# Scores written to PSUM in the key order of V's rows, with the permutation taken out of the normalisation

## The chip, the cores and the metric

The kernel runs on one core of one Trainium2 chip. The metric is the device time of one execution in microseconds. Times quoted are medians of runs in the fast state; ratios are the mean time of one kernel's fast runs over the mean of the other's fast runs of the same rounds, so they are not quite the ratio of the medians that stand beside them. Runs of one execution (called "one look") have no interval.

Names used below: PE is TensorE, ACT is ScalarE, DVE is VectorE, POOL is GpSimd, SP issues the loads. PV is the product of the probabilities with V, QP the Q projection; an evacuation copies a result out of PSUM. `L436` is line 436 of the kernel. In the profiles, SPq or ACTq is an engine's sequencer, and "issue" is time in which an engine waited for nothing that the profile shows.

## The reference

Two independent attention blocks, A and B, whose outputs are put side by side:

```python
def ref(x, k_cache, v_cache, wq, wo):       # x (16, 64, 640), caches (16, 32, 512, 128)
    q = (x @ wq).reshape(B, Sq, 32, 128).transpose(0, 2, 1, 3)
    scores = jnp.einsum("bhqd,bhkd->bhqk", q, k_cache) * 128 ** -0.5
    p = softmax(scores, axis=-1)            # over 512 keys
    o = jnp.einsum("bhqk,bhkd->bhqd", p, v_cache)
    return o.transpose(0, 2, 1, 3).reshape(B, Sq, 32 * 128) @ wo
```

All arrays are bf16. K and V of both blocks make up 268 MB of the 292 MB read.

The scores of these inputs are tiny (standard deviation near 0.001, worked out from the input scales), so the softmax is nearly uniform, and the comparison with the reference does not notice keys in a wrong order.

## The kernel before

Each pack is four heads of two batch rows; 128 packs follow each other. The kernel gives each engine a list of instructions, set out by hand, which it goes through in that order. Four pieces matter.

```python
# Loads: a partition of K holds 16 consecutive keys, a partition of V holds 4 consecutive keys.
src = K[...].rearrange("h (p t) d -> (h p) (t d)", t=16)     # key = 16 * k + j
src = V[...].rearrange("g (p t) d -> p g t d", p=128)        # key = 4 * p + t

def em_KT(e, op):       # DVE: 32x32 block transposes of K, 1024 fp32 (pairs of bf16) per partition
    dst = kt_ring[:, n % NKT, b].rearrange("p t j k two -> p (t j k two)").bitcast(F32)
    ins = e.transpose(dst, kn_ring[:, n % NK, b, :].bitcast(F32))

def em_S(e, op):        # PE: scores, 32 matmuls in four waves (f) of eight array tiles (b, i)
    for f in range(4):
        for b in range(2):
            for i in range(4):
                last = e.matmul(ps[64 * b:64 * b + 64, i, :], qs_ring[rows, n % NQ, f, b, :],
                                kt_ring[rows, n % NKT, b, :, f // 2, :, f % 2],
                                start=(f == 0), stop=(f == 3), tile_position=(32 * i, 64 * b))

def em_NM(e, op):       # POOL: p / rowsum, and the keys into the order of V's rows
    src = p_ring[:, h % NP, :].rearrange("q (th tl k) -> q th tl k", th=4, tl=4)
    dst = pn_ring[:, h % NPN, :].rearrange("q (tl k th) -> q th tl k", tl=4, th=4)
    ins = e.tensor_scalar(dst, src, recip[...], 1.0, ALU.mult, ALU.mult)
# ... (exponential on ACT, reciprocal and most evacuations on DVE, transposes of p, PV and projection on PE)
```

With j = 4 th + tl, a key is 16 k + 4 th + tl. The scores leave PE in the order (th, tl, k). V's row 4 k + th of chunk tl needs the order (tl, k, th). The normalisation therefore reads one contiguous row of 512 bf16 and writes neighbours four elements (8 bytes) apart.

## Time and profile before

951 us (median 950.95 of 4 runs, 948.79 to 951.89).

| | before |
|---|---|
| profiled span | 946.3 us |
| busy: PE / DVE / ACT / POOL | 741.5 / 577.9 / 418.6 / 700.1 us |
| start of the first normalisation | 47.4 us |
| distance of packs in the steady part | 6.73 us |
| the eight packs at the switch from block A to B | 77.2 us together |
| normalisation, start to start in a pair | 1.25 us |

The distance of packs is the time from the first normalisation of one pack to that of the next, taken from the trace's start times. Share of busy time alone would point at PE (78%) as much as at POOL (74%). The chain that ended last decides. This is its summary by engine on the page of before:

```profile
POOL 72%; DVE 11%; PE 10%; SPq 4%; issue 2%; DMA 1%; ACT 0%; ACTq 0%
```

And this is that chain in order of time in the steady part of before (columns: start us, length us, what; one pack is the stretch from one four-fold normalisation to the next):

```profile
307.69 5.17 POOL pn_ring L436 x4
312.87 0.05 issue
312.92 0.63 PE ps L444 x8
313.55 0.02 issue
313.57 0.69 DVE pT_ring L449
314.26 0.08 DVE recip L429
314.35 0.08 issue
314.43 5.17 POOL pn_ring L436 x4
```

Four normalisations take 5.17 us. Then the probabilities of the last two heads are transposed on PE, copied by DVE, and only then does DVE come to the reciprocal of the next pack, since it is behind that copy in DVE's list. From one to the next it is 6.74 us. The groups of before that the change touches (line, engine, operation, shapes, count; busy us, mean ns; idle time before and its cause):

```profile
L436 POOL TENSOR_SCALAR pn_ring<-p_ring,recip 128x512 bf16<-128x512 bf16 x512 | 662.9, 1417 | 195.9 <-DVE recip L429 195.9
L403 PE MATMUL ps<-kt_ring,qs_ring 32*64 32x512 bf16 x4096 | 146.9, 398 | 1.9 <-DVE kt_ring L393 1.9
```

The mean of 1417 ns for a normalisation contains overlap with the next one; start to start it is 1.25 us.

### The profile page before, as it was taken

How to read it: one execution, taken by the hardware profiler on the slowest of the kernel's cores; microseconds unless marked ns; L12 is line 12 of the kernel's file. 1: busy time of each engine (PE TensorE's matmuls, PEld its weight loads, DVE VectorE, ACT ScalarE, POOL GpSimd, SP SyncE). 2: the span in 40 equal slices, each digit the busy share in tenths (PEclk: the TensorE clock that was granted, in tenths of full speed). 3: DMA queues.
4: the chain of work that ended last, by engine and by line, in shares of the span. 5: the costliest groups of instructions: out<-in, count | busy, mean ns of one | idle time of the engine just before them, and what ended most of it. 6: DMA issues, size and time to landing. Idle time of an engine off the chain costs nothing.

```text
span 946.3 us, 31604 instructions
## 1 busy us (share of the span) xinstructions
PE 741.5 (78%) x13905; PEld 524.2 (55%) x13905; DVE 577.9 (61%) x902; ACT 418.6 (44%) x1313; POOL 700.1 (74%) x550
## 2 busy tenths in 40 slices
PE   3077888888888888887677888888888888888884
PEld 2055556565656565655455565656565656555553
DVE  2056666666666666666445666666666666666663
ACT  1034545444544444444333454545454444454442
POOL 2099777777777778788777878787878777777774
PEclk9999999999999999999989999999999999999999
DMA  9999999989999998997579999999999999999820
GB/s 332 366 368 342 367 325 307 336 305 330 318 327 312 318 331 307 324 362 271 199 236 377 373 375 378 376 372 327 327 315 319 325 311 332 305 334 317 300 86 12
DMA packets 195729, 296.79 MB, mean 314 GB/s; under 512 B 9216, under 2 KB 162816, under 8 KB 195584
## 3 DMA queue, kind: packets, MB, share of 16 engines
q1 hardware_dynamic: 193280, 292.06, 89.4%
q10 hardware_dynamic: 2304, 2.62, 0.8%
q8 instruction: 112, 1.84, 0.8%
q14 instruction: 33, 0.27, 0.1%
HBM read 292.03 MB, written 2.62 MB: 311 GB/s over the span
## 4 chain that ended last, share of the span: by engine, by line
POOL 72%; DVE 11%; PE 10%; SPq 4%; issue 2%; DMA 1%; ACT 0%; ACTq 0%
POOL pn_ring L436 68%; DVE pT_ring L449 9%; PE ps L444 8%; POOL wqp_sb L357 2%; POOL wqp_sb L356 1%; SPq L349 1%; SPq L335 1%; DVE recip L429 1%; PE ps L380 1%; DMA ws_ring<-in_A_wq_dram 1%; SPq L342 1%; DVE kt_ring L393 1%; DVE qs_ring L386 0%; PE ps L403 0%; PE ps L460 0%
## 5 line engine op out<-in xcount | busy, mean ns | idle before, releaser
L436 POOL TENSOR_SCALAR pn_ring<-p_ring,recip 128x512 bf16<-128x512 bf16 x512 | 662.9, 1417 | 195.9 <-DVE recip L429 195.9
L416 ACT ACTIVATE p_ring<-ps 128x512 bf16<-128x512 f32 x512 | 304.0, 596 | 358.7 <-PE ps L403 358.7
L449 DVE COPY pT_ring<-ps 128x1024 bf16<-128x1024 bf16 x256 | 177.1, 692 | 294.7 <-PE ps L444 294.7
L393 DVE STREAM_TRANSPOSE kt_ring<-kn_ring 128x1024 f32<-128x1024 f32 x256 | 315.9, 1234 | 7.5 <-DMA kn_ring<-in_A_k_cache_dram 7.5
L444 PE MATMUL ps<-ident,pn_ring 128*128 128x128 bf16 x2048 | 159.9, 221 | 184.6 <-POOL pn_ring L436 184.6
L444 PEld LDWEIGHTS ps<-ident,pn_ring 128*128 128x128 bf16 x2048 | 116.0, 98 | 238.5 <-POOL pn_ring L436 238.1
L460 PEld LDWEIGHTS ps<-pT_ring,v_ring 128*128 128x128 bf16 x4096 | 141.2, 99 | 58.5 <-issue 57.5
L380 PE MATMUL ps<-xT_ring,wqp_sb 128*128 128x128 bf16 x2560 | 170.9, 224 | 2.1 <-POOL wqp_sb L357 1.3
L474 PE MATMUL ps<-wo_sb,oT_ring 128*128 128x512 bf16 x512 | 167.6, 385 | 0.0
L460 PE MATMUL ps<-pT_ring,v_ring 128*128 128x64 bf16 x4096 | 165.1, 194 | 2.7 <-DVE pT_ring L449 1.7
L466 ACT ACTIVATE oT_ring<-ps 128x256 bf16<-128x256 f32 x256 | 98.3, 384 | 143.4 <-PE ps L460 143.4
L380 PEld LDWEIGHTS ps<-xT_ring,wqp_sb 128*128 128x128 bf16 x2560 | 156.8, 115 | 3.3 <-ACT p_ring L416 1.7
L403 PE MATMUL ps<-kt_ring,qs_ring 32*64 32x512 bf16 x4096 | 146.9, 398 | 1.9 <-DVE kt_ring L393 1.9
L386 DVE TENSOR_SCALAR qs_ring<-ps 128x512 bf16<-128x512 f32 x128 | 88.5, 692 | 52.6 <-PE ps L380 52.6
L477 PE MATMUL ps<-wo_sb,oT_ring 128*128 128x128 bf16 x512 | 112.4, 220 | 0.0
L416 ACT ACTIVATION_READ_ACCUMULATOR p_ring<-ps 128x1 f32 x512 | 105.4, 206 | 0.0
L474 PEld LDWEIGHTS ps<-wo_sb,oT_ring 128*128 128x128 bf16 x512 | 50.2, 98 | 64.6 <-ACT oT_ring L466 33.3
L403 PEld LDWEIGHTS ps<-kt_ring,qs_ring 32*64 32x64 bf16 x4096 | 55.5, 104 | 41.6 <-DVE kt_ring L393 2.2
L477 PEld LDWEIGHTS ps<-wo_sb,oT_ring 128*128 128x128 bf16 x512 | 50.5, 99 | 0.0
L356 POOL COPY wqp_sb<-ws_ring 128x1280 bf16<-128x1280 bf16 x16 | 20.3, 1266 | 38.7 <-DMA ws_ring<-in_A_wq_dram 38.7
L429 DVE RECIPROCAL recip<-rowsum 128x2 f32<-128x2 f32 x256 | 35.9, 140 | 4.0 <-ACT p_ring L416 4.0
L357 POOL COPY wqp_sb<-ws_ring 128x1280 bf16<-128x1280 bf16 x16 | 20.2, 1260 | 0.0
(19 smaller groups left out, 39.7 us busy)
## 6 DMA issues: line engine op xcount, KB each, us to landing
kn_ring<-in_A_k_cache_dram SPq DMA_DIRECT2D x128, 512.0 KB, 6.6
v_ring<-in_A_v_cache_dram SPq DMA_DIRECT2D x128, 512.0 KB, 6.1
kn_ring<-in_B_k_cache_dram SPq DMA_DIRECT2D x128, 512.0 KB, 7.0
v_ring<-in_B_v_cache_dram SPq DMA_DIRECT2D x128, 512.0 KB, 6.6
ws_ring<-in_A_wq_dram SPq DMA_DIRECT2D x8, 640.0 KB, 8.0
wo_sb<-in_A_wo_dram SPq DMA_DIRECT2D x8, 640.0 KB, 10.7
ws_ring<-in_B_wq_dram SPq DMA_DIRECT2D x8, 640.0 KB, 4.9
wo_sb<-in_B_wo_dram SPq DMA_DIRECT2D x8, 640.0 KB, 11.3
```

Of the source, the lines that this page charges most:

```text
L380: last = e.matmul(ps[:, 0, f * 128:(f + 1) * 128], w[:, kt, f, :], xT_ring[:, xs, kt, :], start=(kt == 0), stop=(kt == KT - 1))
L386: ins = e.tensor_scalar(qs_ring[:, op.idx % NQ].rearrange("p f b q -> p (f b q)"), ps[:, 0, :], scale, None, ALU.mult)
L393: ins = e.transpose(dst, kn_ring[:, n % NK, b, :].bitcast(F32))
L403: last = e.matmul(ps[64 * b:64 * b + 64, i, :], qs_ring[rows, n % NQ, f, b, :], kt_ring[rows, n % NKT, b, :, f // 2, :, f % 2], start=(f = ...
L416: ins = e.activation(p_ring[:, h % NP, :], ps[:, h % 4, :], ACTF.Exp, scale=1.0, accum_out=rowsum[:, h:h + 1])
L436: ins = e.tensor_scalar(dst, src, recip[:, (h // 2) % NR, h % 2:h % 2 + 1], 1.0, ALU.mult, ALU.mult)
L444: last = e.transpose(pt_ps[:, s, t, :], pn_ring[:, h % NPN, t * 128:(t + 1) * 128], ident[:, :])
L449: ins = e.tensor_copy(pT_ring[:, op.idx % NT].rearrange("p s t q -> p (s t q)"), pt_flat)
L460: last = e.matmul(o_ps[:, col:col + 64], v_ring[:, n % NV, b, 2 * a + s, t, :], pT_ring[:, m % NT, s, t, 64 * b:64 * b + 64], start=(t == ...
L466: ins = e.activation(oT_ring[:, op.idx % NO].rearrange("p s q -> p (s q)"), o_ps, ACTF.Copy)
L474: last = e.matmul(out_ps0, oT_ring[:, m % NO, s, :], wo_sb[:, h, 0:N0], start=(h == 0), stop=(h == H - 1))
L477: last = e.matmul(out_ps1, oT_ring[:, m % NO, s, :], wo_sb[:, h, N0:D], start=(h == 0), stop=(h == H - 1))
```

## The change

The intent is to let POOL read and write contiguous rows, by having PE write the scores to PSUM in V's order already. PE then writes fp32 neighbours four elements (16 bytes) apart.

```diff
-        kt_ring = sb("kt_ring", [128, NKT, 2, 16, 2, 32, 2], BF16)
+        kt_ring = sb("kt_ring", [128, NKT, 2, 4, 4, 2, 32, 2], BF16)      # same bytes, j split
 ... em_KT: the same flat destination
 def em_S
-                        last = e.matmul(ps[64 * b:64 * b + 64, i, :], qs_ring[rows, n % NQ, f, b, :],
-                                        kt_ring[rows, n % NKT, b, :, f // 2, :, f % 2],
+                        dst = ps[64 * b:64 * b + 64, i, :].rearrange("p (tl k th) -> p th tl k", tl=4, th=4)
+                        last = e.matmul(dst, qs_ring[rows, n % NQ, f, b, :],
+                                        kt_ring[rows, n % NKT, b, :, :, f // 2, :, f % 2],
 def em_NM
-            src = p_ring[:, h % NP, :].rearrange("q (th tl k) -> q th tl k", th=4, tl=4)
-            dst = pn_ring[:, h % NPN, :].rearrange("q (tl k th) -> q th tl k", tl=4, th=4)
-            ins = e.tensor_scalar(dst, src, recip[...], 1.0, ALU.mult, ALU.mult)
+            ins = e.tensor_scalar(pn_ring[:, h % NPN, :], p_ring[:, h % NP, :], recip[...], 1.0, ALU.mult, ALU.mult)
```

More of the change, by code (lines that the diff above doesn't have):

```diff
@@ L391, in em_KT @@
             n, b = op.idx
-            dst = kt_ring[:, n % NKT, b].rearrange("p t j k two -> p (t j k two)").bitcast(F32)
+            dst = kt_ring[:, n % NKT, b].rearrange("p th tl j k two -> p (th tl j k two)").bitcast(F32)
             ins = e.transpose(dst, kn_ring[:, n % NK, b, :].bitcast(F32))
@@ L433, in em_NM @@
             h = op.idx
-            src = p_ring[:, h % NP, :].rearrange("q (th tl k) -> q th tl k", th=4, tl=4)
-            dst = pn_ring[:, h % NPN, :].rearrange("q (tl k th) -> q th tl k", tl=4, th=4)
-            ins = e.tensor_scalar(dst, src, recip[:, (h // 2) % NR, h % 2:h % 2 + 1], 1.0, ALU.mult, ALU.mult)
+            ins = e.tensor_scalar(pn_ring[:, h % NPN, :], p_ring[:, h % NP, :], recip[:, (h // 2) % NR, h % 2:h % 2 + 1], 1.0, ALU.mult, ALU.mult)
             return ins, ins
```

## The prediction

> **What bounds the kernel now.** The timeline shows the same pack (four heads of two batches) repeated 128 times, 6.735 us apart for about 115 of them. The chain of waits repeats one loop: four normalisations on Pool (5.17 us: three start-to-start steps of 1.245 us and a last one of 1.42), then PE transposes (0.63), the DVE copy of them (0.69), the reciprocal queued behind that copy on DVE (0.08), about 0.16 of handover. Pool's idle time before the normalisation (195.9 us in the groups) is wholly that handover. 128 x 6.735 = 862 us; the rest is 47 us before the first normalisation and eight packs of 9.1 to 10.1 us around 440 to 515 us, where the second block's weights load. PE is close behind: adding its issue times in one period gives about 5.2 us (scores 1.07, PV 2 x 0.46, transposes 2 x 0.5, QP 1.1, output projection 1.1). DMA runs at up to 376 GB/s after the switch; 2.097 MB per pack at that rate is 5.6 us.
>
> **What the change does.**
> 1. The normalisation loses its stepped output (8 bytes between neighbours). It now takes 1.245 us per 512 elements[...]; Pool's own copies of 1280 elements, output 4 bytes apart, start 1.20 us apart, 0.94 ns per element.[...]
> 2. The score matmuls now write fp32 with 16 bytes between neighbours.[...] Nothing in this trace shows it. I take half rate: four waves of eight tiles go from 0.27 to about 0.43 us, the scores from 1.07 to about 1.75 us per pack. Read side and matmul count stay the same.
> 3. Exp, copies, PV and DMA are unchanged.
>
> **Critical path afterwards.**[...] PE's sum becomes about 5.9 to 6.1. The longest loop: scores 1.75, PV 0.5, transposes 0.65, DVE copy and reciprocal 1.0[...], transposes 0.6 = about 6.25 us. [...]some 0.5 us is kept; PE becomes the bound. 120 x (6.735 - 6.2) = 64 us; start and block switch stay nearly as they are (perhaps 5 us less). **About 880 us, 8 in 10 between 845 and 1000.** Chances: faster by over 2% 0.66, within 2% 0.07, slower by over 2% 0.27.
>
> **What would show each step.** Normalisation mean 1417 ns falling to 650-1000 ns; score matmul busy time 147 us rising to 220-250 us and the score group 1.14 us per pack becoming about 1.85; the period 6.1 to 6.3 us; PE busy over 85%; the chain no longer mostly Pool; Pool idle over 2 us per pack; steady DMA about 340 GB/s.
>
> **What would make it wrong.** If the stepped PSUM write runs at quarter rate, the scores take about 3.5 us, PE's sum is near 7.8 us and the kernel is near 1080 us. If the normalisation does not get faster (its cost is arithmetic, not the step), the longer loop is 7.1 us, about 995 us. If PSUM writes are not slowed, PE and DMA allow 5.6 to 5.8 us, near 825 us. Or the half-rate loops interlock worse than added here.

Terms are missing from the sums: that of the longest loop came to about 6.25 us with a term for two normalisations. From a period of 6.2 us the forecast came to about 880 us. Half rate for a stepped PSUM write is the assumption; nothing in before's trace stood behind it, and after's waves then took 0.43 us.

## The result, and the profile after

859 us (median 858.98 of 4 runs, 857.79 to 859.39). The ratio to before is 0.9034, with a 95% interval of 0.9014 to 0.9053: 9.7% less time.

The chain's summary on the page of after:

```profile
PE 85%; SPq 4%; POOL 4%; DMA 2%; DVE 2%; issue 1%; ACT 0%; ACTq 0%
```

One pack of the chain in order of time, after (columns as above; the lines cut are the output projection, L473 and L476):

```profile
302.40 1.85 PE ps L404 x32
304.25 0.57 PE ps L459 x16
304.82 0.45 PE ps L443 x8
305.27 1.12 PE ps L380 x20
306.39 0.47 PE ps L459 x16
306.85 0.05 issue
...
308.05 0.45 PE ps L443 x8
308.49 1.85 PE ps L404 x32
```

PE hardly waits (it is busy for 19.79 of the 20 us from 300 to 320): scores, PV, transposes, Q projection, PV, output projection, transposes, scores again, 6.09 us later. POOL is no longer in the loop. The same two groups after:

```profile
L435 POOL TENSOR_SCALAR pn_ring<-p_ring,recip 128x512 bf16<-128x512 bf16 x512 | 348.0, 692 | 415.9 <-DVE recip L430 415.5
L404 PE MATMUL ps<-kt_ring,qs_ring 32*64 32x512 bf16 x4096 | 249.0, 628 | 2.0 <-DVE kt_ring L393 1.9
```

The normalisation went from 1.25 to 0.67 us start to start. The scores went from 1.07 us (first score matmul to the next PV) to 1.85 us per pack; their waves start 0.43 us apart in place of 0.24.

Where the 90.3 us of the span came from, by the start times of the normalisations (us):

| | before | after | gained |
|---|---|---|---|
| until the first normalisation | 47.4 | 47.4 | 0.0 |
| five packs in which block A's weights still come | 38.1 | 31.6 | 6.5 |
| steady part of A (52 packs) | 350.1 | 319.1 | 31.0 |
| switch to block B (8 packs) | 77.2 | 60.5 | 16.7 |
| rest of B | 417.4 | 382.0 | 35.4 |
| tail | 16.1 | 15.3 | 0.8 |

So the steady parts gave 66.4 us, and a quarter of the gain came from the two places where weights are prepared.

### The profile page after: what moved, and what is told of

Its sections match the earlier page's. It is cut to its first block, busy times and chain, and to the rows that moved or that the text cites. A ratio compares the mean times of both kernels' runs of the same rounds, so it can differ in the third digit from the quotient of the medians.

```text
span 856.0 us, 31476 instructions
## 1 busy us (share of the span) xinstructions
PE 787.3 (92%) x13777; PEld 521.4 (61%) x13905; DVE 577.1 (67%) x902; ACT 418.7 (49%) x1313; POOL 387.0 (45%) x550
## 4 chain that ended last, share of the span: by engine, by line
PE 85%; SPq 4%; POOL 4%; DMA 2%; DVE 2%; issue 1%; ACT 0%; ACTq 0%
PE ps L404 25%; PE ps L380 16%; PE ps L459 14%; PE ps L443 13%; PE ps L473 10%; PE ps L476 5%; SPq L349 2%; POOL pn_ring L435 1%; DMA v_ring<-in_B_v_cache_dram 1%; SPq L335 1%; POOL wqp_sb L356 1%; POOL wqp_sb L357 1%; DVE kt_ring L393 1%; SPq L342 1%; DMA ws_ring<-in_A_wq_dram 1%
## 5 line engine op out<-in xcount | busy, mean ns | idle before, releaser
L435 POOL TENSOR_SCALAR pn_ring<-p_ring,recip 128x512 bf16<-128x512 bf16 x512 | 348.0, 692 | 415.9 <-DVE recip L430 415.5
L393 DVE STREAM_TRANSPOSE kt_ring<-kn_ring 128x1024 f32<-128x1024 f32 x256 | 315.9, 1234 | 7.3 <-DMA kn_ring<-in_A_k_cache_dram 7.2
L404 PE MATMUL ps<-kt_ring,qs_ring 32*64 32x512 bf16 x4096 | 249.0, 628 | 2.0 <-DVE kt_ring L393 1.9
L459 PEld LDWEIGHTS ps<-pT_ring,v_ring 128*128 128x128 bf16 x4096 | 138.7, 98 | 112.3 <-issue 105.1
L443 PE MATMUL ps<-ident,pn_ring 128*128 128x128 bf16 x2048 | 156.7, 219 | 40.1 <-POOL pn_ring L435 40.1
L380 PE MATMUL ps<-xT_ring,wqp_sb 128*128 128x128 bf16 x2560 | 165.9, 220 | 2.1 <-POOL wqp_sb L357 1.3
L459 PE MATMUL ps<-pT_ring,v_ring 128*128 128x64 bf16 x4096 | 162.5, 193 | 5.3 <-issue 1.9
L443 PEld LDWEIGHTS ps<-ident,pn_ring 128*128 128x128 bf16 x2048 | 122.0, 98 | 54.5 <-POOL pn_ring L435 41.3
L380 PEld LDWEIGHTS ps<-xT_ring,wqp_sb 128*128 128x128 bf16 x2560 | 151.1, 114 | 4.1 <-ACT p_ring L417 2.5
L473 PE MATMUL ps<-wo_sb,oT_ring 128*128 128x512 bf16 x384 | 132.3, 384 | 0.0
L476 PE MATMUL ps<-wo_sb,oT_ring 128*128 128x128 bf16 x512 | 112.5, 220 | 6.9 <-issue 0.2
L404 PEld LDWEIGHTS ps<-kt_ring,qs_ring 32*64 32x64 bf16 x4096 | 63.1, 123 | 84.5 <-issue 69.3
L473 PEld LDWEIGHTS ps<-wo_sb,oT_ring 128*128 128x128 bf16 x512 | 50.0, 98 | 64.5 <-ACT oT_ring L465 33.7
L476 PEld LDWEIGHTS ps<-wo_sb,oT_ring 128*128 128x128 bf16 x512 | 50.4, 98 | 0.0
```

The costliest lines, as they stand in the source:

```text
L380: last = e.matmul(ps[:, 0, f * 128:(f + 1) * 128], w[:, kt, f, :], xT_ring[:, xs, kt, :], start=(kt == 0), stop=(kt == KT - 1))
L404: last = e.matmul(dst, qs_ring[rows, n % NQ, f, b, :], kt_ring[rows, n % NKT, b, :, :, f // 2, :, f % 2], start=(f == 0), stop=(f == 3), t ...
L435: ins = e.tensor_scalar(pn_ring[:, h % NPN, :], p_ring[:, h % NP, :], recip[:, (h // 2) % NR, h % 2:h % 2 + 1], 1.0, ALU.mult, ALU.mult)
L443: last = e.transpose(pt_ps[:, s, t, :], pn_ring[:, h % NPN, t * 128:(t + 1) * 128], ident[:, :])
L459: last = e.matmul(o_ps[:, col:col + 64], v_ring[:, n % NV, b, 2 * a + s, t, :], pT_ring[:, m % NT, s, t, 64 * b:64 * b + 64], start=(t == ...
L473: last = e.matmul(out_ps0, oT_ring[:, m % NO, s, :], wo_sb[:, h, 0:N0], start=(h == 0), stop=(h == H - 1))
```

## The experiments

Theory. (a) POOL pays for the distance of the elements that it writes (1.25 us with 8 bytes in before, 0.67 us contiguous in after). (b) PE pays when it writes PSUM with neighbours that do not lie side by side in 8 bytes (0.24 us per wave in before, 0.43 in after). (c) Both sit in loops that run through several engines, so POOL's gain counts until PE's own list is the longest thing. Rivals: POOL's old cost came from the pattern having several runs or dimensions; PE is slow on any pattern that is not contiguous, or slow in proportion to the step; the slower scores fit into slack and cost nothing. Kernels that were sent off together ran on the same chip with before (medians 949.5 to 951.1 us).

### The two costs apart: slow_slow and fast_fast

The change couples two effects. Two kernels complete the table of the four combinations.

```diff
 slow_slow: after, with the old stepped normalisation (keys permuted twice, wrong on purpose)
+            src = p_ring[...].rearrange("q (th tl k) -> q th tl k", th=4, tl=4)
+            dst = pn_ring[...].rearrange("q (tl k th) -> q th tl k", tl=4, th=4)
 fast_fast: after, with contiguous scores (no permutation at all, wrong on purpose)
-                        dst = ps[...].rearrange("p (tl k th) -> p th tl k", tl=4, th=4)
+                        dst = ps[...].rearrange("p (th tl k) -> p th tl k", tl=4, th=4)
```

> Stepped score writes as after, with the normalisation stepped as before (the result is wrong on purpose: the order is permuted twice). Theory: the two costs are separate and the score group's extra 0.78 us is not hidden, because with slow normalisations one loop runs through both (scores 1.85, PV and transposes 1.2, copy and reciprocal 0.85, two normalisations 2.66, transposes 0.5): period about 7.0 us, time 980 to 1000 us; normalisations stay 1.245 us start to start. Rival: the old Pool loop had slack for slower scores, so nothing is lost: period 6.735 us, about 951 us.

> Contiguous score writes and contiguous normalisation, with the permutation left out (result wrong on purpose). Theory: the whole 0.78 us of PE time comes from the step of the PSUM write; score waves return to 0.24 us, PE's sum falls to about 5.3 us and the DMA queue (2.15 MB per pack at 376 GB/s, 5.7 us) binds: period about 5.7 us, 805 to 825 us. Rival: something else than PE's scores holds the period at 6.1 us (859 us).

| | contiguous scores | stepped scores |
|---|---|---|
| stepped normalisation | before: 951 us, 6.73 us per pack | slow_slow: 987.2 us, 7.09 |
| contiguous normalisation | fast_fast: 824.2 us, 5.83 | after: 859 us, 6.10 |

The table gives medians of the times and of the distance of packs. slow_slow is slower than before (ratio 1.0389, interval 1.0360 to 1.0418); fast_fast has ratio 0.8672 (0.8633 to 0.8710). This is the chain of slow_slow in order of time, one pack:

```profile
299.28 2.65 POOL pn_ring L437 x2
301.93 0.05 issue
301.98 0.62 PE ps L445 x8
302.60 1.85 PE ps L404 x32
304.45 0.57 PE ps L461 x16
305.02 0.46 PE ps L445 x8
...
305.51 0.69 DVE pT_ring L450
306.20 0.08 DVE recip L430
...
306.37 2.66 POOL pn_ring L437 x2
```

With slow normalisations the longest loop is another one than before: two normalisations, transposes, scores, PV, transposes, copy, reciprocal. Its sum is 7.09 us. In before the same loop was 0.78 us shorter, 6.3 us, and stayed hidden behind the 6.73 us of the POOL loop. So of the scores' 0.78 us, 0.36 us per pack surfaces, and the rival that they would fit into slack falls. fast_fast shows the other side: without the step the waves are 0.24 us again, and the stepped PSUM write costs after 35 us (859 less 824).

fast_fast does not settle at one distance. Packs lie between 5.06 and 8.73 us (the longest at the switch of blocks), with 5.31 us as the usual value of packs that do not wait for data. The GB/s row of its page reads 366 to 380 in 33 of 40 slices, the queue of the loads is counted as 100.4% of the time of 16 DMA engines, and it wins 0.26 us per pack in the median where PE's list became 0.78 us shorter. The rate alone decides little, since after reads 366 to 380 in 23 of its slices too. A kernel with a PE list between the two (`pe_patterns`, below, scores of 1.47 us per pack) says more: its packs come every 5.71 us as a rule, and it took 829.7 us. So the last 0.4 us per pack by which PE's list got shorter brought only some 5 us in all. I take fast_fast to be limited by DMA for most of the span. That is an inference from these numbers; no run here moved fewer bytes.

### Where else the permutation could go: read_step, v_order4, dve_order

Each of these keeps the result right and the normalisation contiguous, and moves the permutation to another place.

```diff
 read_step: PE reads K with 1024 bytes between neighbours and writes PSUM contiguously
+                        dst = ps[...].rearrange("p (tl k th) -> p tl k th", tl=4, th=4)
-                                        kt_ring[rows, n % NKT, b, :, :, f // 2, :, f % 2],
+                                        kt_ring[...].rearrange("p th tl k -> p tl k th"),
 v_order4: V's rows are loaded in the order (th, k), by four DMAs of 32 partitions
+            src = V[...].rearrange("g (k th t) d -> th k g t d", k=32, th=4)
+            for th in range(4):
+                ins = e.dma_start(v_ring[32 * th:32 * th + 32, n % NV, b], src[th])
+                        dst = ps[...].rearrange("p (tl th k) -> p th tl k", tl=4, th=4)
 dve_order: DVE's transposes write fp32 with 16 bytes between neighbours, the rest is contiguous
+            dst = dst.rearrange("p (j tl k th) -> p th tl j k", j=2, tl=4, k=32)
+                        dst = ps[...].rearrange("p (tl k th) -> p tl k th", tl=4, th=4)
```

> Right result: the permutation is moved to the score matmuls' read of K from SBUF (neighbours 1024 bytes apart), PSUM is written contiguously. If only the PSUM side is sensitive to a step: waves of 0.24 us and the time of the fast_fast run, near 815 us. If PE also reads a stepped row slowly: waves of 0.43 us or more, 859 us or above. I lean to the second[...].

> Right result: the permutation is moved to the load of V (four DMAs of 32 partitions in place of one of 128; the rows moved stay 1 KB), so scores and normalisation are both contiguous. Theory: as fast_fast, 805 to 830 us, DMA bound, over 3% faster than after. Rival: the four smaller DMAs and their issue time cost more than PE gains, 860 us or above.

> Right result: the permutation is moved to DVE's 32x32 transposes of K, which write fp32 elements 16 bytes apart, so that scores read and write, and the normalisation reads and writes, neighbours at their former distance, and all loads stay whole. Theory: if DVE writes that step at its old pace (1.234 us each, DVE then 4.5 us per pack), everything but DMA has slack and the time is that of fast_fast, 815 to 835 us, some 4% under after. Rival: DVE slows on a 16-byte step as Pool and PE do; at twice 1.234 us DVE needs about 7 us per pack and the kernel about 960 us.

| | median us | ratio to before (95%) | what became slow |
|---|---|---|---|
| read_step | 1080.6 | 1.1365 (1.1340 to 1.1390) | score waves 0.88 us |
| v_order4 | 1217.9 (one run of four, slow, left out) | 1.2804 (1.2741 to 1.2866) | DMA: 244 GB/s in the mean |
| dve_order | 856.9 | 0.9025 (0.9005 to 0.9045) | K's transposes 2.03 us |

The groups that were hit, first of read_step, then of dve_order:

```profile
L404 PE MATMUL ps<-kt_ring,qs_ring 32*64 32x512 bf16 x4096 | 479.8, 1056 | 1.9 <-DVE kt_ring L393 1.9
```

```profile
L394 DVE STREAM_TRANSPOSE kt_ring<-kn_ring 128x1024 f32<-128x1024 f32 x256 | 519.8, 2031 | 7.1 <-DMA kn_ring<-in_A_k_cache_dram 7.1
```

read_step: a read with 1024 bytes between neighbours costs PE more than a write with 16: a wave of 0.88 us against 0.43. No run reads at a distance in between, so where the cost sets in stays open. Before read neighbours 4 bytes apart, and a wave is 3.7 times as long here as before's 0.24 us. Why the distance costs this much is not shown.

dve_order falls between theory and rival. DVE did slow, but by a factor of 1.6, not 2, and the time is that of after: PE's 0.78 us were exchanged for 0.8 us in each of DVE's two transposes per pack. The loop is now Q projection, its evacuation, the second transpose, scores, PV and transposes, 6.05 us.

v_order4 refuted my theory for it. The loads broke it, and two kernels asked why.

### Why four DMAs of 32 partitions are slow: v_split_g and v_split_p

```diff
 v_split_g: four DMAs by head, each over 128 partitions, rows in the old order (wrong order of keys)
+                ins = e.dma_start(v_ring[:, n % NV, b, th], src[:, th])
 v_split_p: four DMAs by partition, 32 each, rows in the old order (wrong order of keys)
+                ins = e.dma_start(v_ring[32 * th:32 * th + 32, n % NV, b], src[32 * th:32 * th + 32])
```

> As v_order4, but the four DMAs for V are cut by head: each reaches all 128 partitions, rows in the old order (order wrong on purpose). If v_order4 was slow because each DMA reached only 32 partitions: 820 to 850 us, DMA at 350 GB/s or more. If it was slow by the number of DMAs: about 1200 us.

> As v_order4, but the four DMAs for V take 32 partitions each with the rows in the old order in memory (order of keys wrong on purpose). If 32 partitions per DMA are the cause: about 1200 us and 245 GB/s as v_order4. If the permuted row order in memory is the cause: 820 to 850 us.

v_split_g took 822.4 us and v_split_p 1232.7 us (one look each). The GB/s rows of their pages, v_split_g first:

```profile
GB/s 328 364 372 367 378 378 374 378 361 376 372 372 372 380 376 377 379 373 371 362 317 376 375 375 375 359 372 375 381 376 373 353 364 377 377 380 367 368 354 67
```

```profile
GB/s 286 293 304 270 272 251 234 222 248 228 225 223 232 235 231 246 236 229 228 246 238 254 229 256 257 239 254 227 249 228 225 257 264 239 259 230 234 247 217 104
```

Both split V into four DMAs of 128 KB, and v_split_g takes no longer than fast_fast, which has one DMA of 512 KB in place of the four (822.4 us and 362 GB/s in the mean, against 824.2 and 361), so neither the number of DMAs nor their size is the cause. Both leave the rows in their old order, so the order is not the cause either: 32 partitions per DMA are, with 241 against 362 GB/s in the mean while K is still loaded over 128 partitions. The runs show that the partitions per DMA matter, not why.

### What a step costs on each engine: pe_patterns, pool_patterns, pairs

To separate "any step", "size of the step" and "neighbours side by side", two kernels rotate patterns and are read by start-to-start times; `pairs` then uses one pattern throughout. All give a wrong order.

```diff
 pe_patterns: pattern (f + n) % 4 of the score write
+   0: "p (th tl k) -> p th tl k"                  contiguous
+   1: "p (tl k th) -> p th tl k"                  step of 16 bytes
+   2: "p (tx tl k ty) -> p tx ty tl k"            step of 8 bytes
+   3: "p (tl kx th ky) -> p th tl kx ky", ky=2    pairs (8 bytes) that hop 32 bytes
 pool_patterns: pattern (h // 2) % 8 of the normalisation, for example
+   2: qv = qv.rearrange("q (k c) -> q c k", c=4)  write step of 8 bytes
+   5: pv = pv.rearrange("q (k c) -> q c k", c=4)  read step of 8 bytes
 pairs: all score writes as pattern 3
```

> Score writes in four patterns in rotation over the accumulation steps and packs (result wrong on purpose), each read from the start-to-start time of its wave of eight matmuls: contiguous, step of 16 bytes, step of 8 bytes, and pairs of neighbours (8 bytes) that hop 32 bytes. Theory[...]: contiguous and pairs 0.24 us, both steps 0.43 us. Rival 1 (any non-contiguous pattern is slow): pairs 0.43 us too. Rival 2 (the cost grows with the step): 8 bytes near 0.24 to 0.33 us, 16 bytes 0.43 us.

> Normalisations in eight patterns in rotation over the pairs of heads (result wrong on purpose), each read from the start-to-start time of a pair: contiguous; write steps of 4, 8 and 16 bytes; write of 32-element runs that hop; read steps of 8 and 16 bytes; read and write steps of 8 bytes. Theory (byte step of the write): contiguous 0.68, runs 0.68, 4 bytes 0.68 to 0.8, 8 bytes 1.245, 16 bytes 1.245 us. Rival 1 (any pattern that is not one run takes a slow path): runs and 4 bytes 1.245 too. Rival 2 (reads behave alike): read step 8 bytes 1.245[...].

> As after, but all score writes go in pairs of neighbours (8 bytes) that hop 32 bytes (order wrong on purpose). The mixed run left open whether a wave of pairs costs as little as a contiguous one. Theory[...]: waves 0.24 to 0.27 us throughout and the time of fast_fast, about 825 us. Rival (pairs only looked fast beside slow waves): waves near 0.43 us and 859 us.

POOL, one look (977.5 us in all); start to start of the two normalisations of a pair, median:

| write / read of 512 bf16 | us |
|---|---|
| contiguous / contiguous | 0.666 |
| runs of 32 elements that hop / contiguous | 0.666 |
| step 4 bytes / contiguous | 0.787 |
| step 8 bytes / contiguous | 1.243 |
| step 16 bytes / contiguous | 2.170 |
| contiguous / step 8 bytes | 0.704 |
| contiguous / step 16 bytes | 1.163 |
| step 8 bytes / step 8 bytes | 1.244 |

So the rival of several runs falls (runs that hop take the 0.666 us of contiguous rows), and the byte step of the write is the cause: the change's 0.58 us per normalisation are all of it. It grows with the step: 0.12 us at 4 bytes, 0.58 at 8, 1.50 at 16, where I had expected no more than at 8. All of these writes are bf16, so whether bytes or elements count is not told apart. Two of these pairs, as the timeline of POOL in pool_patterns shows them (columns: start us, length us, the instructions; both instructions of a pair merged). The first is contiguous, the second writes with a step of 4 bytes:

```profile
301.97 1.36 POOL L457 TENSOR_SCALAR pn_ring<-p_ring,recip 128x512 bf16<-128x512 bf16 x2 [1.82 <-DVE recip L430]
304.21 1.63 POOL L457 TENSOR_SCALAR pn_ring<-p_ring,recip 128x512 bf16<-128x512 bf16 x2 [0.89 <-DVE recip L430]
```

A merged pair also counts the second instruction's own length, so 1.36 us corresponds to 0.67 us start to start. Rival 2 had a read step of 8 bytes as slow as a write step, at 1.245 us; it takes 0.704 us, 0.04 over contiguous.

PE, start to start of waves. In the mixed kernel the second and third waves had medians of 0.22 to 0.23 us contiguous, 0.39 at 16 bytes, 0.43 at 8 bytes, 0.27 for pairs; at 16 bytes the uniform kernel has 0.43 in place of this 0.39, which I put down to the waves beside it (not shown), so I take uniform kernels as the cleaner measure: 0.24 us contiguous (before), 0.43 us at 16 bytes (after), 0.24 us for pairs (median starts of the four waves 0, 0.25, 0.48 and 0.72 us). `pairs` took 822.8 us (one look), as fast_fast. Its group of scores, to be set beside the 398 ns of before and the 628 ns of after:

```profile
L405 PE MATMUL ps<-kt_ring,qs_ring 32*64 32x512 bf16 x4096 | 155.4, 397 | 15.4 <-issue 12.2
```

So both rivals fall: it is not any non-contiguous pattern, and not the size of the step, since 8 bytes (in the mixed kernel alone) is no better than 16. What matters in these runs is whether two neighbours lie side by side in 8 bytes: 0.24 us per wave in `pairs`, as in contiguous rows, against 0.43 us in after.

### The permutation split between DVE and PE: half_half

If DVE's transposes keep their 1.234 us with neighbours 8 bytes apart (with 16 they took 2.03 us), and pairs are enough for PSUM (0.24 us per wave in `pairs`), each engine can do half of the permutation without loss. th is split into (tx, ty).

```diff
-        kt_ring = sb("kt_ring", [128, NKT, 2, 4, 4, 2, 32, 2], BF16)
+        kt_ring = sb("kt_ring", [128, NKT, 2, 2, 4, 2, 32, 2, 2], BF16)
-            dst = kt_ring[:, n % NKT, b].rearrange("p th tl j k two -> p (th tl j k two)").bitcast(F32)
+            dst = kt_ring[:, n % NKT, b].rearrange("p tx tl j k ty two -> p (tx tl j k ty two)").bitcast(F32)
+            dst = dst.rearrange("p (tx c ty) -> p tx ty c", tx=2, ty=2)
-                        dst = ps[64 * b:64 * b + 64, i, :].rearrange("p (tl k th) -> p th tl k", tl=4, th=4)
+                        dst = ps[64 * b:64 * b + 64, i, :].rearrange("p (tl k tx ty) -> p tx tl k ty", tl=4, tx=2, ty=2)
-                                        kt_ring[rows, n % NKT, b, :, :, f // 2, :, f % 2],
+                                        kt_ring[rows, n % NKT, b, :, :, f // 2, :, :, f % 2],
```

> Right result: the permutation is split. DVE's transposes of K interleave two blocks (fp32 written 8 bytes apart[...]), and the score matmuls write pairs of neighbours (8 bytes) that hop 16 bytes. Theory: the pairs run at full rate on PE as in the run with pairs (waves of 0.24 us), DVE's transposes stay near 1.234 us[...], and the kernel is DMA bound at 820 to 830 us, 4% under after. Rival: DVE slows on any step (1.6 us or more for a transpose): DVE then needs about 5.3 us per pack and the loop through transposes, scores and QP about 5.6 us, 830 to 850 us; pairs that hop 16 bytes may also cost PE more than pairs that hop 32.

> The changed kernel itself beside half_half on one chip: 856 to 861 us. half_half should be under it by 30 us or more.

half_half took 824.5 us (823.79 to 826.37, ratio to before 0.8677, 0.8659 to 0.8696), beside 858.9 us for after on the same chip: 4.0% less again (824.52 over 858.92). Its groups:

```profile
L436 POOL TENSOR_SCALAR pn_ring<-p_ring,recip 128x512 bf16<-128x512 bf16 x512 | 349.6, 695 | 381.3 <-DVE recip L431 381.3
L394 DVE STREAM_TRANSPOSE kt_ring<-kn_ring 128x1024 f32<-128x1024 f32 x256 | 316.3, 1236 | 7.4 <-DMA kn_ring<-in_A_k_cache_dram 7.3
...
L405 PE MATMUL ps<-kt_ring,qs_ring 32*64 32x512 bf16 x4096 | 152.3, 393 | 15.7 <-issue 13.4
```

All three engines run at the pace that they have without a step (692, 1234 and 398 ns are the values elsewhere). The kernel is right, has no permutation whose cost shows, and equals fast_fast, which has no permutation at all. For DVE the reason stays open: a transpose takes 1.236 us with a write step of 8 bytes, 2.031 us with 16 (dve_order) and 1.234 us contiguous, and no run shows why.

### What happened at the switch of blocks

No kernel was needed for this; the two traces show it. Around 440 to 515 us POOL also prepares the second block's Q weights, two copies of 1.2 us per pack. The chain of before in this part, in order of time:

```profile
472.38 2.15 PE ps L380 x20
...
476.66 1.43 POOL pn_ring L436
478.09 1.06 POOL wqp_sb L356
479.15 1.20 POOL wqp_sb L357
480.35 1.38 POOL pn_ring L436
```

And that of after:

```profile
442.64 1.13 PE ps L380 x20
...
445.78 0.69 POOL pn_ring L435
446.47 1.19 POOL wqp_sb L356
447.66 1.20 POOL wqp_sb L357
448.86 0.68 POOL pn_ring L435
```

Five times in before the chain takes the loop that it takes in after (in before's first packs there, 9.11 us each, it runs through all four normalisations and the two copies): Q projection, then on DVE (in the lines cut) its evacuation, a transpose of K and the reciprocal, then a normalisation, the two copies, a second normalisation, and transposes on PE. It went from 10.04 to 7.56 us: 1.44 us from the two normalisations and 1.02 us from the Q projection, which took 2.15 us in before and 1.13 in after. The profile shows why the latter in its granted clock: before, in the window of 460 to 480 us, and after, in 442 to 462 us (columns: window, length, busy us and count of each engine, clock, DMA share, GB/s):

```profile
460.00:480.00 20.00, 14.06 (x216) 11.13 (x216) 9.23 (x14) 6.35 (x21) 15.16 (x13) 0.83 0.67 224
```

```profile
442.00:462.00 20.00, 17.23 (x297) 11.67 (x308) 12.61 (x21) 8.45 (x27) 12.67 (x16) 1.00 1.01 348
```

The mean hides the worst of it: in the Q projection alone (472.3 to 474.6 us) before's granted clock is 0.50, which fits its nearly doubled time. PE's longest wait in that part is 3.1 us in before and 1.3 us in after, where the clock reads 1.00. What made before's clock fall, and whether the waits have to do with it, is not shown by a run.

## Why the prediction was right

- The mechanism was right: the chain moved from POOL (72%) to PE (85%), and the period fell from 6.73 to 6.10 us, where 6.1 to 6.3 was said. The time, 859 us, lies in the stated range of 845 to 1000, 21 us below the point of 880.
- Normalisation: its mean was to fall from 1417 ns to 650 to 1000, and 692 came (0.67 us start to start). Its cause, the byte step of the write, is shown by the patterns: 1.24 us at a write step of 8 bytes, 0.67 contiguous. A read step of 8 bytes costs little (0.70 us).
- Scores: half rate was taken; the waves are 0.43 us as said. The group grew from 1.07 to 1.85 us where 1.75 was said, and busy time was 249.0 us where 220 to 250 was said. The half was a guess: nothing in before's trace gave a size, so that it came is luck. That neighbours side by side in 8 bytes escape the cost is shown by the pairs (0.24 us per wave).
- The longest loop was given as 6.25 us, through two normalisations. slow_slow shows this loop at 7.09 us with 2.65 us for the two; with after's 1.36 us it is about 5.8 us, and PE's own list, 6.09 us, binds. The prediction's sum for PE, 5.9 to 6.1 us, was right.
- One term was mis-sized: "start and block switch stay nearly as they are (perhaps 5 us less)". They gave 23.2 us (6.5 and 16.7). The switch is a loop through two normalisations, not a stretch limited by loads, and the clock did not fall any more (1.00 in after's window of 442 to 462 us, 0.83 in before's of 460 to 480). The steady part was given as 64 us and gave 66.4, by two errors that cancel: 120 packs at 0.535 us were counted, and there were 114 at 0.58.
- The second listed way to fail ("the longer loop is 7.1 us, about 995 us") is what slow_slow measured: 7.09 us and 987.2 us. The bound by PE and DMA without PSUM cost ("5.6 to 5.8 us, near 825 us") is what fast_fast measured: 5.83 us and 824.2 us.
- Predicted signs: Pool idle over 2 us per pack is right (415.9 us over 128 packs, 3.2 us each); PE busy over 85% is right (92%); steady DMA near 340 GB/s was too low: its GB/s row reads 336 to 380 in the steady slices (347 in the mean over the whole span).

## What to carry to other kernels

In these runs the permutation was not free or dear as such; each engine had its own distance at which it got dear. POOL's normalisation went from 0.67 us to 0.79 at a write step of 4 bytes and 1.24 at 8; PE's score wave from 0.24 us to 0.43 when single fp32 were written to PSUM 16 bytes apart, and stayed at 0.24 in pairs; DVE's transpose stayed at 1.24 us with 8 bytes and took 2.03 with 16. So ask which engine can absorb it in runs or pairs before moving it whole from one engine to another. Here moving it whole gained 9.7% and splitting it between two engines, each at a step that costs it nothing, gained 13.2%. When two costs are exchanged, add up every loop with the new durations, the starting and switching stretches too: here the loop that bound afterwards was not the one that was relieved.
